# Linformer attention and a gated FFN on one core: the value projection of 14 of 16 token blocks by seven products of half-size matrices

## The chip, the cores and the metric

One NeuronCore of a Trainium2 chip runs the whole program in one launch. The metric is the device time of one execution in microseconds (us). The engines are TensorE (PE in the profile, its weight loads PEld), VectorE (DVE), ScalarE (ACT), GpSimd (POOL) and SyncE (SP); POOL and SP also issue the transfers (DMAs).

## The reference

Attention with K and V projected along the sequence to 64 rows, then a gated feed-forward layer; in the kernel's terms:

```python
k_proj = np.einsum('ks,bhsd->bhkd', E, k)          # 8 batches, 8 heads, 1024 tokens, 64 wide
v_proj = np.einsum('ks,bhsd->bhkd', F, v)
attn = softmax(q @ k_proj.T / 8)                   # over the 64 projected rows
x = (attn @ v_proj).transpose(0, 2, 1, 3).reshape(8192, 512)
gate = 1.0 / (1.0 + np.exp(-(x @ w_gate)))         # 512 -> 1536
out = (gate * (x @ w_val)) @ w_out                 # 1536 -> 512
```

Inputs and output are float32; the matmuls run on bf16 operands with float32 sums.

## The kernel before, in words

The 8192 tokens are 16 **blocks** of 512, two to a batch. xT holds the attention output of a batch transposed (four chunks of 128 rows, two blocks), hT the hidden layer of a block (twelve chunks m of 128 rows by 512 tokens), wG, wV and wO the weights.

For each m, `mstep` makes four matmuls of 512 columns for the gate and four for the value, each group into a PSUM bank of its own. `gate` has ACT take tanh of half the gate sum into sig, and DVE make (sig + 1) x value into hT; the missing factor 0.5 comes with the output.

The output projection of blocks 1 to 14 is made by **seven products** instead of eight (Winograd's form of Strassen's scheme): hT and wO are cut into two by two parts, sums of parts (`s_sums` into hS and in place in hT, `t_sums` into wT) are multiplied, and partial results are read out of the running sums in PSUM by `keep_snap` (ACT) and `add_snap` (DVE). `first_products` makes five products into two banks, `last_products` the other two. Blocks 0 and 15 use the straight `oproj`.

The attention of batch b+1 is cut into pieces (`scores`, `mixed`, `outputs` and so on) that are placed at fixed spots among the msteps of batch b. exp goes to eT; the sums over it come as a matmul with a pattern (dsel); DVE makes reciprocals (`rec`) into rden; `gather` moves them by four small DMAs on SP into rows of rrow (the memory of eT); `spread` has POOL broadcast each row over the partitions into rb, sixteen instructions per batch; `mul` multiplies xu by rb into xT on DVE. K, V and q of batch b+2 are loaded on POOL's queue; q and the projected K are transposed by DMAs on SP.

The order of every engine's work is the order in which the program emits it. `Plan.add` finds for each operation the writers and readers of the keys it names, and the engine waits for their semaphores; a PSUM bank is one key, so its users on different engines take turns. Between matmuls there is no wait on PE itself. `Ring` hands banks out in turn: four for the FFN, four for attention.

Of the kernel before, what the change touches and what calls it, by code (L numbers as in the profile page):

```python
# [7 lines left out]
ALU = mybir.AluOpType  # L8
# [4 lines left out]
P = 128  # L13
# [105 lines left out]
def bass_linformer_attn__then__ffn_glu_sigmoid_kernel(  # L119
# [18 lines left out]
    with contextlib.ExitStack() as es:  # L138
# [5 lines left out]
        count = sbuf("count", [P, P], FP32)  # L144
        quad = sbuf("quad", [P, 1], FP32)
        row_f = sbuf("row_f", [P, 1], FP32)
        pats = sbuf("pats", [P, 4, 32], FP32)
        rows = sbuf("rows", [P, 4, 32], FP32)
        half = sbuf("half", [P, 2], FP32)
        identf = sbuf("identf", [P, P], FP32)  # L150
        ident = sbuf("ident", [P, P], BF16)
        dsel = sbuf("dsel", [P, 2, 2, 32], BF16)
        dsel8 = sbuf("dsel8", [P, 2, 4, 32], BF16)
        bsel8 = sbuf("bsel8", [P, 4, 2, 64], BF16)
        bsel8f = sbuf("bsel8f", [P, 4, 2, 64], FP32)
# [5 lines left out]
        KV = [sbuf(f"KV{i}", [P, H, S // P * DH], BF16) for i in range(2)]  # L161
        kp = sbuf("kp", [P, NR, DH], BF16)
# [5 lines left out]
        rden = sbuf("rden", [P, 512], FP32)  # L168
        rhi = sbuf("rhi", [P, 512], BF16)
        rhl = sbuf("rhl", [P, 512], BF16)  # L170
# [4 lines left out]
        rb = sbuf("rb", [P, 8, 512], FP32)  # L175
# [6 lines left out]
        sig = [sbuf(f"sig{i}", [P, 512], FP32) for i in range(3)]  # L182
# [4 lines left out]
        snap = [EF[:, 0:512], EF[:, 512:1024], sbuf("snap2", [P, 512], FP32)[:, :]]  # L187

# [28 lines left out]
        ffn, att = Ring(FB), Ring(AB)  # L217

# [119 lines left out]
        def constants():  # L338
# [61 lines left out]
            for t, k, m, w in ((dsel8, "dsel8", 8, 4), (dsel, "dsel", 4, 2)):  # L400
# [131 lines left out]
        def half_unit(hf, ring):  # L532
# [86 lines left out]
            def bc(R):  # L619
# [17 lines left out]
                def keep(g):  # L637
                    act(
                        rb[:, 2 * R + g, :],
                        bank[bks[g]][:, :],  # L640
                        [],
                        [("rb", 2 * R + g)],
                        b=bks[g],
                    )
# [17 lines left out]
            def xo(R):  # L662
# [14 lines left out]
                for g in range(2):  # L677
                    n = 2 * R + g
                    if hf:
                        act(xu[:, n, :], bank[bks[g]][:, :], [], [("xu", n)], b=bks[g])  # L680
                    elif R == 0:
                        scale(R, g, bank[bks[g]], rb[:, n, :], [("rb", n)], bks[g])
                if hf == 0 and R == 1:
                    for r in (2, 3):
                        for g in range(2):
# [5 lines left out]
                                    rb[:, 2 * R + g, cc],  # L691
                                    ALU.mult,
                                ),
                                [("rb", 2 * R + g)],
# [57 lines left out]
        def keep_vd(bk):  # L752
            for g in range(2):
                act(
                    vpD[64 * g : 64 * g + 64, :, :].rearrange("p h d -> p (h d)"),
                    bank[bk][64:128, :],
                    [],
                    [("vpD", h, g, R) for h in range(2) for R in range(2)],
                    b=bk,
                )  # L760

        def attention(b):
# [39 lines left out]
            def den():  # L802
                bk = att.next()
                for rnd in range(2):
                    for j in range(4):
                        n = 4 * rnd + j
                        mm(
                            bk,
                            bank[bk][32 * j : 32 * j + 32, :],
                            dsel[:, n % 2, rnd, :],  # L810
                            eT[:, n, :],
                            [("dsel", n % 2), ("eT", n)],
                            start=(rnd == 0),
                            stop=(rnd == 1),
                            tp=(0, 32 * j),
                        )
                den_bank.append(bk)

# [9 lines left out]
            def den8():  # L828
                bk = att.next()
# [51 lines left out]
            def gather():  # L881
                for i in range(4):
                    add(
                        "SP",
                        lambda e, i=i: e.dma_start(rrow[::32, i, :], rden[i::32, :]),
                        r=[("rden", c, R) for c in range(4) for R in range(2)],
                        w=[("rrow", i)] + [("eT", 2 * i + x) for x in range(2)],
                        dma=f"rrow{i}",
                    )

            def spread(rnd):
                for j in range(4):
                    n = 4 * rnd + j
                    for c, parts in ((1, P), (0, 64)):
# [4 lines left out]
                            r=[("rrow", 2 * rnd + c)]  # L899
                            + [("eT", 4 * rnd + 2 * c + x) for x in range(2)],  # L900
                            w=[("rb", n)],
# [21 lines left out]
            def mul(r, g, bk=None):  # L923
# [9 lines left out]
                    [("xu", n)] + ([("rb", n)] if bk is None else []),  # L933
# [13 lines left out]
            def scores():  # L947
                f, a0, a1 = two(ffn), two(att), two(att)
                order = (0, 1, 2) if b == 1 else (2, 0, 1)
# [15 lines left out]
            def outputs():  # L965
# [4 lines left out]
                if 2 < b + 1 < B:  # L970
                    held["kv"] = att.next()
                    kv(b + 1, held["kv"])
                den8() if b == 1 else den()
# [3 lines left out]
            if b == 1:  # L977
# [13 lines left out]
            return [  # L991
                scores,
                lambda: exp_one(1, held["sc"]),
                mixed,
                lambda: keep_x(1, held["x"]),
                outputs,
                lambda: (keep_x(3, held["x"]), rec(1)),
                lambda: (rec(2), keep_kd(held["kv"]) if b + 1 < B else None),
                lambda: (rec(3), gather(), keep_vd(held["kv"]) if b + 1 < B else None),
                lambda: (spread(0), spread(1)),  # L1000
                lambda: mul2(0),
                lambda: mul2(1),
                lambda: mul2(2),
                lambda: mul2(3),
            ]
# [50 lines left out]
        def gate(blk, m, pg, pv):  # L1056
# [3 lines left out]
                sg[:, :], bank[pg][:, :], [], [("sig", M % 3)], b=pg, func=AF.Tanh, scale=0.5  # L1060
# [4 lines left out]
                    sg[:, :],  # L1065
# [5 lines left out]
                [("sig", M % 3)],  # L1071
# [4 lines left out]
        def oproj(blk, tt, pb, cols=((0, DM),)):  # L1076
            o = ost[:, tt, :]
            t = 2 * (2 * (blk % 2) + tt % 2) + tt // 2
            for n, (c0, c1) in enumerate(cols):
                if n:  # L1080
                    pb = ffn.next()
# [17 lines left out]
                )  # L1099
                add(  # L1100
# [24 lines left out]
        def s_sums(blk, n, ms):  # L1125
# [11 lines left out]
            dve(  # L1137
                lambda e: e.tensor_tensor(o, a, b, op),  # L1138
                [k for x in r.split() for k in part(blk, x, up)],
                [k for k in part(blk, w, up)],  # L1140
# [32 lines left out]
        def keep_snap(n, bk):  # L1173
            act(snap[n], bank[bk][:, :], [], [("snap", n)], b=bk, scale=0.5)
# [23 lines left out]
        def first_products(blk):  # L1198
            a, c = ffn.next(), ffn.next()
# [5 lines left out]
            for ms in ((0, 3), (3, 6)):  # L1205
                s_sums(blk, 4, ms)
# [5 lines left out]
            add_snap(2, c, 1, 1)  # L1212

        def last_products(blk):
# [6 lines left out]
            ffn.next(), ffn.next()  # L1221
            for tt in (2, 3, 0, 1):
# [6 lines left out]
                )  # L1229

# [61 lines left out]
        def sums(blk, m):  # L1292
            if m >= 9 and 1 <= blk < 2 * B - 1:
                s_sums(blk, m - 8, (0, 3))
            if m <= 2 and blk >= 2:
                s_sums(blk - 1, m + 1, (3, 6))
            if blk == 2 and m <= 3:
                t_sums(m)

        for b in range(B):  # L1300
            todo = []
            for blk in (2 * b, 2 * b + 1):
                ms = [[m] for m in range(NF)]
                if blk <= 1:
                    ms = [[0, 1]] + ms[2:]
                gaps = {11: [0, 1, 2, 3]} if blk == 1 else {}
                for m in ms:
                    if len(m) == 2:
                        todo.append(
# [89 lines left out]
```

The softmax here doesn't subtract the row's maximum and nothing guards it: scores larger than these inputs give would overflow.

## Time and profile before

| | |
|---|---|
| three runs | 546.61, 546.85, 547.0 us; median 546.85 |
| the profiled execution | 547.47 us, its span from first to last instruction 545.4 us |
| granted TensorE clock | 1.0 |
| wide matmuls of gate and value | 768 each, mean record 379 ns (they overlap) |
| POOL broadcasts into rb | 96, 77.1 us busy |
| DVE gates (L1063) | 192, 130.6 us busy |
| ACT tanh (into sig) | 192, 116.1 us busy |
| DVE sums for hS and hT (L1138) | 112 of 128x768 bf16, about 65 us busy |
| DMA | 56.09 MB, mean 103 GB/s |

A group of instructions is given by line, engine, operation, written and read tiles, and shape (partitions x elements). Matmul records overlap, so their pitch is read from start to start. Idle time of an engine that is not the one that sets the end costs nothing. Line 227 is the helper that records every matmul, line 231 the one for every ACT instruction.

### The profile page before, as it was taken

What the parts mean: (1) busy time and instruction counts of PE and PEld (TensorE: products, weight loads), DVE (VectorE), ACT (ScalarE), POOL (GpSimd) and SP (SyncE); (2) the same over time, 40 slices, a digit from 0 to 9 for tenths busy, and PEclk for the clock granted to TensorE, in tenths of its full rate; (3) what the DMA queues carried; (4) which work ended last, traced back from release to release, by engine and by line L of the source; (5) the groups of instructions that cost most, each with busy time, mean ns of one, the idle gap of its engine ahead of it and who ended that gap; (6) DMA issues with size and microseconds to landing.
All of it is one profiled execution on the core that took longest, in us unless ns stands there. A gap on an engine that the chain in (4) does not pass through costs nothing.

```text
span 545.4 us, 8923 instructions
## 1 busy us (share of the span) xinstructions
PE 530.7 (97%) x3504; PEld 298.7 (55%) x3561; DVE 305.5 (56%) x499; ACT 232.1 (43%) x414; POOL 113.5 (21%) x148
## 2 busy tenths in 40 slices
PE   5999999999999999999999999999999999999998
PEld 4544445646565474644647465564656547474654
DVE  4645386346863559437583466734785375834432
ACT  2654823465335633365333753346533562323330
POOL 9310200103800055000830019000350007100000
PEclk9999999999999999999999999999999999999999
DMA  9999998983795117960286502953020202001022
GB/s 159 200 195 201 163 209 176 153 178 49 148 201 127 31 21 150 152 156 11 79 137 131 121 12 78 185 144 59 13 78 1 78 0 81 2 7 72 1 77 78
DMA packets 76570, 56.09 MB, mean 103 GB/s; under 512 B 34704, under 2 KB 68240, under 8 KB 76528
## 3 DMA queue, kind: packets, MB, share of 16 engines
q0 software_dynamic: 33984, 29.89, 35.4%
q1 hardware_dynamic: 42544, 25.63, 18.6%
q8 instruction: 28, 0.46, 0.4%
q14 instruction: 14, 0.11, 0.1%
HBM read 60.29 MB, written 16.78 MB: 141 GB/s over the span
## 4 chain that ended last, share of the span: by engine, by line
PE 93%; DMA 2%; DVE 1%; ACT 1%; issue 1%; POOL 1%; POOLq 0%
PE pF L227 88%; PE pA L227 5%; DMA KV<-in_v_dram 2%; DVE hT L1063 0%; DVE rden L822 0%; POOL KV L245 0%; POOL Qb L245 0%; ACT xu L231 0%; ACT vpD L231 0%; ACT sig L231 0%; ACT eT L231 0%; ACT kpd L231 0%; DVE rden L602 0%; DVE hS L1138 0%; DVE xT L651 0%
## 5 line engine op out<-in xcount | busy, mean ns | idle before, releaser
L1063 DVE SCALAR_TENSOR_TENSOR hT<-sig,pF 128x512 bf16<-128x512 f32 x192 | 130.6, 681 | 118.9 <-PE pF L227 75.1
L227 PE MATMUL pF<-xT,wV 128*128 128x512 bf16 x752 | 195.6, 379 | 1.2 <-DVE hT L1063 0.3
L227 PE MATMUL pF<-xT,wG 128*128 128x512 bf16 x729 | 191.2, 379 | 3.1 <-issue 1.3
L231 ACT ACTIVATE sig<-pF 128x512 f32<-128x512 f32 x192 | 116.1, 605 | 171.2 <-PE pF L227 146.6
L896 POOL PARTITION_BROADCAST rb<-eT x96 | 77.1, 864 | 279.6 <-DMA eT<-rden 274.5
L227 PEld LDWEIGHTS pF<-xT,wV 128*128 128x128 bf16 x768 | 75.0, 98 | 90.9 <-DVE hT L1063 1.0
L227 PEld LDWEIGHTS pF<-xT,wG 128*128 128x128 bf16 x768 | 72.6, 98 | 88.6 <-issue 9.0
L227 PE MATMUL pF<-wO,hT 128*128 128x256 bf16 (+3 forms) x610 | 80.8, 287 | 0.1
L227 PEld LDWEIGHTS pF<-wO,hT 128*128 128x128 bf16 x612 | 59.2, 98 | 19.7 <-issue 0.8
L1183 DVE SCALAR_TENSOR_TENSOR ost<-pF,EF 128x512 f32<-128x512 f32 x28 | 19.4, 692 | 51.4 <-PE pF L227 48.8
L227 PE MATMUL pF<-wT,hT 128*128 128x256 bf16 x336 | 41.2, 273 | 0.0
L927 DVE TENSOR_TENSOR xT<-xu,rb 128x512 bf16<-128x512 f32 x48 | 40.3, 878 | 0.0
L227 PE MATMUL pF<-wT,hS 128*128 128x256 bf16 x336 | 39.0, 273 | 0.3 <-ACT EF L231 0.3
L231 ACT ACTIVATE EF<-pF 128x512 f32<-128x512 f32 x28 | 16.7, 597 | 47.0 <-PE pF L227 46.9
L227 PEld LDWEIGHTS pF<-wT,hT 128*128 128x128 bf16 x336 | 32.9, 98 | 6.8
L227 PEld LDWEIGHTS pF<-wT,hS 128*128 128x128 bf16 x336 | 32.8, 98 | 4.3 <-ACT EF L231 0.6
L822 DVE RECIPROCAL rden<-pA 128x128 f32<-128x128 f32 x26 | 24.6, 950 | 9.5 <-PE pA L227 9.5
L1183 DVE SCALAR_TENSOR_TENSOR ost<-pF,snap 128x512 f32<-128x512 f32 x14 | 9.7, 692 | 35.6 <-PE pF L227 25.0
L231 ACT ACTIVATE xu<-pA 128x512 f32<-128x512 f32 x46 | 25.2, 617 | 1.1 <-PE pA L227 1.1
L231 ACT ACTIVATE snap<-pF 128x512 f32<-128x512 f32 x14 | 8.4, 597 | 28.3 <-PE pF L227 28.3
L231 ACT ACTIVATE eT<-pA 128x512 bf16<-128x512 f32 x35 | 19.3, 622 | 1.0 <-PE pA L227 1.0
L231 ACT ACTIVATE eT<-pF 128x512 bf16<-128x512 f32 x29 | 15.8, 594 | 8.3 <-PE pF L227 8.2
(93 smaller groups left out, 268.5 us busy)
## 6 DMA issues: line engine op xcount, KB each, us to landing
out_dram<-ost SPq DMA_DIRECT2D x63, 256.0 KB, 2.4
Qb<-in_q_dram POOLq DMA_DIRECT2D x7, 1024.0 KB, 17.8
KV<-in_k_dram POOLq DMA_DIRECT2D x7, 1024.0 KB, 9.8
KV<-in_v_dram POOLq DMA_DIRECT2D x7, 1024.0 KB, 14.0
wO<-in_moe_w_out_dram POOLq DMA_DIRECT2D x1, 1536.0 KB, 11.9
wG<-in_moe_w_gate_dram POOLq DMA_DIRECT2D x5, 256.0 KB, 18.2
wV<-in_moe_w_val_dram POOLq DMA_DIRECT2D x5, 256.0 KB, 18.8
KV<-in_k_dram POOLq DMA_DIRECT2D x2, 512.0 KB, 8.8
```

The costliest lines, as they stand in the source:

```text
L227: return add("PE", lambda e: e.matmul(o, lhsT, rhs, **kw), r=r, x=[("bank", b)])
L231: return add("ACT", lambda e: e.activation(o, i, func, scale=scale), r=r, w=w, x=x)
L822: lambda e: e.reciprocal(rden[:, cc], bank[bk][:, cc]),
L896: lambda e, n=n, i=2 * rnd + c, j=j, parts=parts: e.partition_broadcast(rb[0:parts, n, :], rrow[32 * j : 32 * j + 1, i, :], channels=parts),
L927: lambda e: e.tensor_tensor(xT[s][:, r, :, 256 * g : 256 * g + 256], xu[:, n, :].rearrange("p (f c) -> p f c", f=2), y.rearrange("p (f c) ...
L1063: lambda e: e.scalar_tensor_tensor(hT[blk % 2][:, m, :], sg[:, :], 1.0, bank[pv][:, :], ALU.add, ALU.mult,),
L1183: lambda e: e.scalar_tensor_tensor(o, bank[bk][:, :].rearrange("p (j c) -> p j c", j=2), 0.5, snap[n].rearrange("p (j c) -> p j c", j=2), ...
```

## The change

**Values by seven products.** From block 2 on the value projection too is cut in two by two by two: two halves of the tokens (256 each), two halves of the 512 inputs, two halves of the 1536 outputs. Sums of parts of wV are made once by `vt_sums` (T1 in place in wV, T2 to T4 in the new vT); sums of parts of xT per block by `xs_sums` into xS, both on DVE. `v_product` is one product for a pair of m: four matmuls of 256 columns.

**Units.** The work is in units K of four gate groups (`g_step`) and seven value products (`v_pieces`), six units per batch, each laid out in nine slots: `p3` of the unit before, `p1`, gate, `p26`, gate, `p57`, gate, `p4`, gate of the next unit. Two PSUM banks a and c of a unit take running sums; ACT copies them to vsnap (`v_snap`), DVE adds the other bank (`v_add`), and `hidden` on DVE makes hT from sig and vsnap, in one of four cases from PSUM. Banks come from free lists (FF, AA) instead of rings.

**Sums on GpSimd.** S1 to S3 of the output products of blocks 2 to 14, which DVE made before, are made on POOL: three instructions of 128x1024 elements after the second unit of a block (four of the six chunks of a half), three of 128x512 after the third; for block 2b both come ahead of the `spread` of the same pass on POOL's queue, for block 2b+1 the first comes behind it. A key q7 keeps them apart from broadcasts. S4 stays on DVE.

**Attention.** Its parts get spots at slots (u, j), u the unit and j the slot: `scores` at (0, 0), `mixed` at (1, 0), `outputs` at (3, 0), with the later ACT copies one bank at a time (`late`). The denominators of all batches use the layout that batch 1 had (`den8`: two `rec` of 128 columns instead of four, eight gather DMAs instead of four). `mul` sits in the output products at (5, 0), two before and one behind them, and at (5, 4).

**Memory.** rb shares the memory of the K and V tiles; constants used only at the start, and others, share that of vT.

Batch 0 stays as it was, apart from four straight `oproj` of block 0 at its end, where the sums for weights and block 1 are made.

```diff
+        KVs = sbuf("KVs", [P, 2, H, S // P * DH], BF16)
+        KV = [KVs[:, i, :, :] for i in range(2)]
+        rb = (
+            KVs[:, :, :, :].rearrange("p w h c -> p (w h c)").bitcast(FP32)
+            .rearrange("p (n c) -> p n c", n=8)
+        )
...
             def gather():
-                for i in range(4):
+                for m in range(8):
...
-                            w=[("rb", n)],
+                            w=[("rb", n), ("KV", n // 4, n % 4 // 2)],
...
+            def outputs3():
+                f, a0 = FF.two(), AA.two()
+                xo_one(2, f)
+                xo_one(3, a0)
+                bd = AA.take()
+                den8(bd)
+                if b + 1 < B:
+                    held["kv"] = AA.take()
+                    kv(b + 1, held["kv"])
+                for g in range(2):
+                    x_half(2, g, f)
+                    FF.append(f[g])
+                later("A0", x_half, 3, a0, AA)
+                rec(0)
+                rec(1)
+                AA.append(bd)
+                gather()
+                spread(0)
+                spread(1)
...
-            for ms in ((0, 3), (3, 6)):
-                s_sums(blk, 4, ms)
+            s_sums(blk, 4, (0, 6))
+            hook(0)
             product(blk, a, "S2", "T2")
             keep_snap(1, a)
             product(blk, c, "S1", "T1", True)
             product(blk, a, "A21", "T3")
             keep_snap(2, a)
             add_snap(2, c, 1, 1)
+            hook(1)
...
+        def hidden(K, half_, tok, x, r, b=None):
...
+            o = hT[blk % 2][:, m : m + 2, cc]
+            dve(
+                lambda e: e.scalar_tensor_tensor(
+                    o,
+                    sg[:, :, cc],
+                    1.0,
+                    x.rearrange("p (j c) -> p j c", j=2),
+                    ALU.add,
+                    ALU.mult,
+                ),
...
+        def v_snap(n, bk):
+            act(vsnap[n][:, :], bank[bk][:, :], [], [("vsnap", n)], b=bk)
+
+        def v_add(n, bk):
+            o = vsnap[n][:, :]
+            dve(
+                lambda e: e.tensor_tensor(o, bank[bk][:, :], o, ALU.add),
...
+            def p1():
+                held_v["a"] = a = FF.take()
+                v_product(blk, q, a, "A11", "B11", start=True)
+                v_snap(0, a)
+
+            def p26():
+                a = held_v["a"]
+                held_v["c"] = c = FF.take()
+                v_product(blk, q, c, "A12", "B21", start=True, stop=True)
+                v_add(0, c)
+                v_product(blk, q, a, "S2", "T2")
+                v_snap(1, a)
+                hidden(K, 0, 0, vsnap[0][:, :], [("vsnap", 0)])
+
+            def p57():
+                a, c = held_v["a"], held_v["c"]
+                v_product(blk, q, c, "S1", "T1", start=True)
+                v_product(blk, q, a, "S3", "T3")
+                v_snap(2, a)
+                v_add(2, c)
+
+            def p4():
+                a = held_v["a"]
+                v_product(blk, q, a, "A22", "T4", stop=True)
+                hidden(K, 0, 1, bank[a][:, :], [], b=a)
+                FF.append(a)
+                hidden(K, 1, 1, vsnap[2][:, :], [("vsnap", 2)])
+
+            def p3():
+                c = held_v["c"]
+                v_product(blk, q, c, "S4", "B22", stop=True)
+                v_add(1, c)
+                FF.append(c)
+                hidden(K, 1, 0, vsnap[1][:, :], [("vsnap", 1)])
...
+        for i, fn in zip((12, 14, 15, 16, 17, 18, 19, 19, 20, 21, 22), attention(1)):
+            put(i, fn)
...
+        put(22, lambda: [s_sums(1, n, (3, 6)) for n in (1, 2, 3)])
+        put(22, lambda: (vt_sums(3), vt_sums(1), vt_sums(2), vt_sums(4)))
+        put(23, lambda: (t_sums(0), t_sums(1)))
+        put(24, lambda: (t_sums(2), t_sums(3)))
+        put(25, lambda: [xs_sums(2, n) for n in (1, 2, 3, 4)])
...
+            if b > 1:
+                on(0, 2, lambda: pool_sums(o0, (4, 6)))
+            on(2, 4, lambda: pool_sums(o1, (0, 4)))
+            on(3, 0, lambda: pool_sums(o1, (4, 6)))
+            if b + 1 < B:
+                on(5, 4, lambda: pool_sums(o1 + 1, (0, 4)))
+            on(2, 0, lambda: [xs_sums(o1 + 1, n) for n in (1, 2, 3, 4)])
+            k0 = 0 if b == 1 else 2
+            on(k0, 0, lambda: first_products(o0))
+            on(k0, 2, lambda: last_products(o0))
...
+                on(5, 0, lambda: first_products(o1, hook))
+                on(5, 4, lambda: (mul(3, 0), mul(3, 1)))
+                on(5, 7, lambda: [xs_sums(o1 + 2, n) for n in (1, 2, 3, 4)])
...
+            on(5, 2, lambda: last_products(o1))
+            if b + 2 < B:
+                on(0, 4 if b == 1 else 2, lambda: (load_k(b + 2), load_v(b + 2), load_q(b + 2)))
+                on(3, 4, transpose_q)
```

(o0 is block 2b - 1 and o1 block 2b of the pass for batch b; `hook` multiplies r = 0 and 1 at its first call, r = 2 at its second.)

## The prediction

> **What bounds the kernel now.** I read the busy shares and the chain first, then the sums over single batch pairs, then the order of instructions in one quiet stretch, then how long one line's instructions last.
>
> ```profile
> PE 530.7 (97%) x3504; PEld 298.7 (55%) x3561; DVE 305.5 (56%) x499; ACT 232.1 (43%) x414; POOL 113.5 (21%) x148
> PE 93%; DMA 2%; DVE 1%; ACT 1%; issue 1%; POOL 1%; POOLq 0%
> 187.92:252.51 64.59, 64.12 (x409) 36.59 (x416) 37.91 (x58) 28.92 (x52) 15.36 (x19) 1.00 0.50 101
> 252.51:317.10 64.59, 64.11 (x409) 36.59 (x416) 37.93 (x58) 28.92 (x52) 15.37 (x19) 1.00 0.50 101
> ```
>
> The last two lines are two passes of the loop over batches: the length, then the busy time of PE, PEld, DVE, ACT, POOL, then the granted clock. The pass is 64.59 us each time and PE is busy for 64.1 of it at full clock. So TensorE sets the end, and it hardly waits. Only fewer columns through PE can help, and every wait that PE gets is paid in full.
>
> The price of columns, and of a hand-over, is in the timeline of a quiet stretch (start, length, engine, line):
>
> ```profile
> 280.46 1.03 PE L227 MATMUL pF<-xT,wG 128*128 128x512 bf16 x4
> 281.32 1.03 PE L227 MATMUL pF<-xT,wV 128*128 128x512 bf16 x4
> 281.58 0.60 ACT L231 ACTIVATE sig<-pF 128x512 f32<-128x512 f32 x1 [1.13 <-PE pF L227]
> 282.19 1.03 PE L227 MATMUL pF<-xT,wG 128*128 128x512 bf16 x4
> 282.46 0.69 DVE L1063 SCALAR_TENSOR_TENSOR hT<-sig,pF 128x512 bf16<-128x512 f32 x1 [0.57 <-PE pF L227]
> 287.37 2.78 PE L227 MATMUL pF<-wO,hT 128*128 128x256 bf16 x24
> 289.99 0.27 PE L227 MATMUL pF<-wT,hS 128*128 128x256 bf16 x1
> ```
>
> Four 512-column matmuls start every 0.862 us (280.46, 281.32, 282.19), so a wide matmul costs 0.2155. Twenty-four 256-column ones take 289.99 - 287.37 = 2.62 us, 0.109 each: half width costs half. After a group ends, ACT starts 0.26 us later (281.32 to 281.58) and DVE 0.27 (282.19 to 282.46).
>
> **The gain.** A block's values were 48 wide matmuls, 48 x 0.2155 = 10.34 us. Seven products of 2 x 6 matmuls of 256 columns are 84 x 0.109 = 9.16. That is 1.18 less per block, 14 blocks: **-16.5 us**. Gate, output products, scores and K/V projection keep their columns. The denominators go from 8 wide matmuls to 16 of half width, four side by side as before: no change.
>
> **What ACT and DVE get.** Per pass of two blocks there are six units; each adds three snapshots on ACT (0.60) and three additions on DVE. DVE instructions of 128x512 that follow one another start every 0.60 us. ACT goes from 28.9 to 28.9 + 18 x 0.60 = 39.7 us, DVE from 37.9 by +18 x 0.60, +8 x 0.35 for xS (a 128x768 bf16 sum lasts 0.55, so by elements 0.37 and less in a row), -12 x 0.47 for the sums that leave, -2 x 0.9 for two reciprocals, to about 44. Both fit in a pass of some 62.2 us. What matters is the order inside a unit: 28 x 0.109 + 16 x 0.2155 = 6.5 us of PE.
>
> **Hand-overs in a unit.** The tightest is `p4`: it adds to bank a after `v_snap(2)` has read it, covered by one gate group, 0.862 us. The snapshot costs 0.26 + 0.60, and PE has started 0.05 us after an ACT or DVE end where it waited (96.15 to 96.20): 0.91, so 0.05 per unit, 42 x 0.05 = 2.1 us. In three units per pass the `late` halves of exp and xu stand ahead of it on ACT and make it about 0.1 more, 18 x 0.1 = 1.8. The others have room: `S1 T1` waits for `v_add(0)`, ready at 2.0, done at 2.7, wanted at 3.0; `p3` for `v_add(2)`, done at 5.5, wanted at 6.1. Together **+4**; from 0 (ACT and PE overlap by that 0.05) to 17, if each unit loses 0.4.
>
> **The seam after batch 0.** The four straight output groups of block 0 last 4 x 2.59 = 10.4 us. Behind the last gate DVE gets there: 8 multiplications by 0.60, 5 sums by 0.47, four `vt_sums` and four `t_sums` of 128x1536 at 0.87 apart (the 0.95 us row), four evictions, four xS sums: 4.8 + 2.4 + 7.0 + 2.4 + 1.5 = 18, and waits for the first eviction make it 19. `add_snap(0)` of the next output products queues behind that and ends at 19.8; PE wants its bank at 10.4 + 0.6 + 0.9 + 3 x 1.31 = 15.8. **+4**, once; 0 to 6.
>
> **The port.** The sums S1 to S3 go to POOL, and no row of before has a TENSOR_TENSOR there. What POOL does to DVE is in these lines (minimum, median, maximum of a line, then DVE's and POOL's timeline):
>
> ```profile
> L927 DVE TENSOR_TENSOR xT<-xu,rb x48: 681/792/1147, 140.0 to 471.0; 128x512 bf16<-128x512 f32 x48
> L927 DVE TENSOR_TENSOR xT<-xu,pA x8: 677/680/681, 74.1 to 81.3; 128x512 bf16<-128x512 f32 x8
> L1063 DVE SCALAR_TENSOR_TENSOR hT<-sig,pF x192: 624/687/690, 25.3 to 532.4; 128x512 bf16<-128x512 f32 x192
> 269.18 1.97 DVE L927 TENSOR_TENSOR xT<-xu,rb 128x512 bf16<-128x512 f32 x2
> 272.70 2.14 DVE L927 TENSOR_TENSOR xT<-xu,rb 128x512 bf16<-128x512 f32 x2
> 276.16 1.29 DVE L927 TENSOR_TENSOR xT<-xu,rb 128x512 bf16<-128x512 f32 x2
> 268.22 6.21 POOL L896 PARTITION_BROADCAST rb<-eT  x7 [0.16 <-POOL rb L896]
> L896 POOL PARTITION_BROADCAST rb<-eT x96: 794/799/1207, 131.6 to 465.4; - x96
> ```
>
> Two multiplications take 1.29 us when POOL is quiet, 1.97 and 2.14 while broadcasts run (until 274.4); the broadcast itself stretches from 0.80 to 1.21. The same multiplication with one input in PSUM never exceeds 0.681, and the gates, also with one PSUM input, not 0.690. So a DVE instruction with two SBUF inputs and a POOL instruction exclude each other. After the change three of a unit's four `hidden`, all xS sums, S4 and the multiplications by rb are of that kind.
>
> [...]
>
> Price of a sum of 1024 bf16 elements on POOL, D: not below 0.8, the broadcast that writes the same 2 KB per partition; not above 3.2, twice for the elements (1024 for 512) and twice for the second input. By bytes alone 0.8, by elements alone 1.6; I take **1.2**, half way.
>
> Most places have cover. At (2,4) the sums wait for `S1 T1` of the output products (hS is one buffer), which puts them under 8 us of output products where DVE has only PSUM work. The half-size sums at (0,2) and (3,0) run under scores and `outputs`. The spread meets `hidden` six times, 0.3 us each, inside DVE's slack.
>
> The place without cover is slot (5,0), six passes. Counted from there, PE wants `add_snap(2)` done at 9.6 (p3, five output products of 1.31, p1, a gate group, one product) and `v_add(0)` at 12.65. The spread starts late: rec ends 3.9 us after (3,0), eight gather DMAs instead of four at about 0.6 each on SP (four take 2.36 us) put the first broadcast 4.8 us behind it, and 16 x 0.775 plus 2 us of collisions end it at 7.4 after (5,0); then S1 to S3 start. DVE has `hidden` to 2.2, `add_snap(0)` to 3.9, S4 to 5.1, three multiplications to 7.8 among the broadcasts; the fourth waits for S1 (port free 0.3 before its end). With D = 1.2: fourth to 9.2, `add_snap(2)` 9.8 (0.3 late with the hand-over), the next two 10.65 and 12.1 between S2 and S3, `add_snap(1)` and `v_add(0)` 13.3 against 12.95: 0.7 per pass, **+4**. With D = 0.8 nothing is late; 1.6: 1.85, +11; 2.4, midway to the upper bound: 4.2, +25; 3.2: 6.8, +41. Behind the three sums POOL has the next half-size sums and loads, some 9 us of slack later.
>
> **K and V under rb.** Loads of batch b+2 wait for POOL's half-size sums, so go out some 6 us into the pass; V lands 14 us after issue, Q 17.8, and `outputs` wants K and V some 31 us in. Nothing, with 11 us to spare; without that cover PE would stand for the rest of the load. On SP the transposes of q stand behind 2.4 us more of gather, a pass ahead of the scores: nothing.
>
> **Edits without a price.** Four constants of 0.34 us leave DVE at the start, where the chain waits for K and V instead; `keep` writes xu in place of rb. At the end `hidden(1,0)` comes two DVE instructions after p3, 1.5 us, under the first ten matmuls of the straight output group (2.2 us); without them PE would wait that long.
>
> **The sum**, against the profiled execution's span of 545.4: 545.4 - 16.5 + 4 + 4 + 4 = 540.9. The median of the runs, 546.85, is 1.5 above that span: **542.5 us**.
>
> **The rivals.** *Everything is covered*: D near 0.8, no hand-over late, the seam within its slack; 545.4 - 16.5 + 1.5 = 530.4, up to 534. For it: the broadcasts cost PE nothing now. Against: DVE's 19 us of work in 11 at the seam. 0.12.
> *The port decides* (slower): at slot (5,0) POOL's three large sums lock out the multiplications, and PE stands for `add_snap(2)` and `v_add(0)`. The gain is gone once a pass loses (16.5 - 8)/6 = 1.4 us, from D of about 1.5. At 1.6: 549; at 2.4: 563; at the upper bound 579; its likeliest part 549 to 565. For it: the stretched rows; against: POOL's speed is not seen. 0.30.
> *The hand-overs eat it*: seven banks per unit change between PE, ACT and DVE, and 0.4 us lost in each of 42 units is 16.8: 546 to 550, no change or slightly slower. For it: three covers of about 0.86 us; against: ACT's starts are regular to 0.01 us. 0.14, half of it within the measurement.
>
> **How the numbers follow.** Forecast, 534 to 545.7: 0.44. A measurement of this kernel tells 0.2%, 1.1 us, from no change. Faster 0.44 + 0.12 = 0.56, same 0.07, slower 0.30 + 0.07 = 0.37. The range, 531 to 563, leaves out the low end of full cover and a D above 2.4. The forecast's own range is 534 to 546.
>
> **What would show it.** Right: passes of about 62.5 to 64 us, PE busy nearly throughout; POOL TENSOR_TENSOR 128x1024 of 1.2 us; PE's only waits on DVE at (5,0) and the seam. Wrong: a POOL sum above 1.5 us with `xT<-xu,rb` rows of 1.5 us and PE waiting on `ost` or `vsnap`; or ACT's snapshots as PE's releaser in each unit.

## The result, and the profile after

The changed kernel took **578.58 us** (573.99 to 584.19 in four runs) against 546.92 us for the kernel before: 1.0551 times as long, 95% interval 1.049 to 1.0612. Ratios, here and below, leave out executions that took over 1.5% longer than the fastest of their kernel. The forecast of 542.5 us was wrong, and on the wrong side: the kernel got slower. The profiled execution took 578.65 us, its span 576.8.

The page of the changed kernel: busy shares, the granted clock in 40 slices, and the chain that ended last.

```profile
PE 533.1 (92%) x4113; PEld 348.1 (60%) x4113; DVE 401.2 (70%) x577; ACT 300.9 (52%) x540; POOL 263.2 (46%) x226
PEclk9999999988999999899998999999997999999999
PE 71%; DVE 16%; DMA 8%; issue 3%; POOL 1%; SPq 1%; ACT 0%; DVEq 0%; POOLq 0%
```

PE no longer sets the end alone: DVE holds 16% of the chain and DMA 8%, where before they held 1% and 2%. The clock is no longer full throughout: 0.979 in the mean, for 1.000 before, and below 0.9 in five of the 40 slices.

Stretches of about one pass each, from the end of `outputs` in one pass, slot (3, 0), to its end in the next (length, then busy time of PE, PEld, DVE, ACT, POOL, clock, DMA share, GB/s):

```profile
141.76:205.54 63.78, 62.78 (x497) 43.09 (x498) 49.82 (x69) 38.70 (x69) 38.54 (x32) 1.00 0.51 102
205.54:273.06 67.52, 64.43 (x499) 43.65 (x498) 50.15 (x69) 38.60 (x69) 38.02 (x32) 0.97 0.49 97
273.06:341.78 68.72, 63.96 (x497) 43.66 (x498) 51.38 (x69) 38.60 (x69) 37.88 (x32) 0.98 0.49 95
341.78:406.39 64.61, 62.96 (x497) 43.02 (x498) 51.01 (x69) 38.65 (x69) 39.29 (x32) 1.00 0.53 100
406.39:474.91 68.52, 63.62 (x481) 43.40 (x482) 49.99 (x67) 38.33 (x69) 33.29 (x27) 0.95 0.19 50
```

Before, each pass took 64.59. One pass is faster than that, one the same, three are 3 to 4 us slower, at a clock below 1. Ahead of them something else went wrong: block 4's first gate already starts 18.2 us later than before (169.45 for 151.28), of 31.4 at the end.

**A slow pass.** POOL's, DVE's and PE's timelines of the changed kernel around the first gates of block 8 (start, length, engine, line, in brackets the idle time before):

```profile
288.10 7.38 POOL L916 PARTITION_BROADCAST KVs<-eT  x7 [0.19 <-POOL KVs L916]
302.78 2.19 POOL L1226 TENSOR_TENSOR hS<-hT 128x1024 bf16<-128x1024 bf16 x1 [7.29 <-DVE xS L1372]
305.05 2.18 POOL L1226 TENSOR_TENSOR hS<-hS,hT 128x1024 bf16<-128x1024 bf16 x1
307.30 2.18 POOL L1226 TENSOR_TENSOR hT<-hT 128x1024 bf16<-128x1024 bf16 x1
...
302.57 0.42 DVE L1372 TENSOR_TENSOR xS<-xS,xT 128x512 bf16<-128x512 bf16 x1
302.91 2.34 DVE L1372 TENSOR_TENSOR xS<-xT 128x512 bf16<-128x512 bf16 x1
305.17 2.33 DVE L1372 TENSOR_TENSOR xS<-xT,xS 128x512 bf16<-128x512 bf16 x1
307.43 0.68 DVE L1429 TENSOR_TENSOR vsnap<-pF,vsnap 128x512 f32<-128x512 f32 x1
308.14 1.89 DVE L1410 SCALAR_TENSOR_TENSOR hT<-sig,vsnap 128x512 bf16<-128x512 f32 x1
...
302.88 0.61 PE L263 MATMUL pF<-xT,wV 128*128 128x256 bf16 x4
308.16 1.89 PE L263 MATMUL pF<-xT,wG 128*128 128x512 bf16 x4 [4.68 <-DVE vsnap L1429]
```

Read it from the bottom. PE stands 4.7 us until `v_add(1)` (L1429, from 307.43) has freed a bank. That addition is held up by nothing of its own: two xS sums ahead of it take 2.34 and 2.33 us instead of 0.42, each until a POOL sum of 2.18 has ended. POOL's sums stand there because POOL was idle for 7.3 us between its last broadcast (ends 295.5) and its first sum. Had it gone on at once, these three would have ended at about 302.2, when xS begins. The gate's four matmuls then take 1.89 us instead of 1.03: from 308.2 to 311.2 the granted clock is 0.54.

**The first pass.** SP, POOL and PE in the changed kernel's timeline:

```profile
106.39 1.46 SPq L779 DMA_TRANSPOSE kpD<-kpd  x1
...
104.57 0.89 POOL L281 DMA_DIRECT2D KVs<-in_k_dram  x1 [31.96 <-PE pF L263]
...
108.70 0.60 PE L263 MATMUL pF<-xS,wV 128*128 128x256 bf16 x4
115.34 0.64 PE L263 MATMUL pF<-qT,kpD 64*64 64x512 bf16 x4 [6.04 <-DMA kpD<-kpd]
116.77 1.04 PE L263 MATMUL pF<-xT,wV 128*128 128x256 bf16 x4
```

The stretch of that wait and the one behind it, columns as above:

```profile
109.00:115.30 6.30, 0.30 (x3) 0.02 (x1) 1.71 (x3) 0.90 (x2) 0.00 (x0) 0.81 1.21 189
115.30:118.30 3.00, 2.96 (x18) 1.26 (x19) 0.00 (x0) 1.49 (x3) 0.00 (x0) 0.50 1.24 208
```

The scores wait 6.0 us (6.04 in the row) for the small transposition of the projected K. It was issued at 106.39, behind the loads of batch 3 (from 104.57), and landed 8.9 us later; the median of the six is 3.2. In the kernel before it was issued at 94.63 and the loads at 96.72. The clock is then 0.50 for 3 us. Ahead of this lies a wait of 3.51 us for `add_snap(0)` (L1278), and behind it one of 4.72 us for `vsnap`:

```profile
94.09 1.48 PE L263 MATMUL pA<-wT,hS 128*128 128x256 bf16 x12 [3.51 <-DVE ost L1278]
133.56 1.03 PE L263 MATMUL pF<-xS,wV 128*128 128x256 bf16 x4 [4.72 <-DVE vsnap L1429]
```

Waits of PE are given here as the idle time in its rows. Those that the expectations name are up to 0.2 us longer, since they count from where the next matmul could have started.

How long one instruction lasts, by groups of the changed kernel (busy us, mean ns, then idle before them):

```profile
L1226 POOL TENSOR_TENSOR hS<-hT 128x1024 bf16<-128x1024 bf16 x13 | 28.3, 2178 | 117.0 <-PE pA L263 54.2 <-DVE xS L1372 30.2 <-DVE hT L1410 17.8
L1226 POOL TENSOR_TENSOR hT<-hT 128x1024 bf16<-128x1024 bf16 x13 | 29.1, 2240 | 1.0
L1410 DVE SCALAR_TENSOR_TENSOR hT<-sig,vsnap 128x512 bf16<-128x512 f32 x126 | 112.8, 895 | 5.8
L1410 DVE SCALAR_TENSOR_TENSOR hT<-sig,pF 128x512 bf16<-128x512 f32 x42 | 28.9, 687 | 0.7 <-PE pF L263 0.7
```

D, the price of a POOL sum, is 2.2 us, not 1.2. The same `hidden` costs 687 ns with one input in PSUM and 895 in the mean with two in SBUF (731 in e1 below, with no sums on POOL): the lock that the prediction read out of the multiplications. It calls it the port; the rows show that the two engines keep each other out, not by what. DVE has 50 to 51 us of work a pass in the table of stretches, where the prediction had about 44; the lock is part of that (18 `hidden` with two inputs in SBUF a pass, 0.21 us longer each than with one in PSUM, are 3.7 us).

### The profile page after: what moved, and what is told of

It is laid out like the page before. It is cut to its first block, busy times and chain, and to the rows that moved or that the text cites. A ratio compares the mean times of both kernels' runs of the same rounds, so it can differ in the third digit from the quotient of the medians.

```text
span 576.8 us, 10389 instructions
## 1 busy us (share of the span) xinstructions
PE 533.1 (92%) x4113; PEld 348.1 (60%) x4113; DVE 401.2 (70%) x577; ACT 300.9 (52%) x540; POOL 263.2 (46%) x226
## 4 chain that ended last, share of the span: by engine, by line
PE 71%; DVE 16%; DMA 8%; issue 3%; POOL 1%; SPq 1%; ACT 0%; DVEq 0%; POOLq 0%
PE pF L263 50%; PE pA L263 21%; DVE xT L948 5%; DVE xS L1372 4%; DMA Qb<-in_q_dram 3%; DVE vsnap L1429 3%; DMA KVs<-in_v_dram 2%; DVE hT L1410 2%; DMA kpD<-kpd 2%; DVE ost L1278 1%; SPq L741 1%; DMA out_dram<-ost 1%; POOL KVs L281 1%; DVE hT L1226 1%; ACT vsnap L267 0%
## 5 line engine op out<-in xcount | busy, mean ns | idle before, releaser
L1429 DVE TENSOR_TENSOR vsnap<-pF,vsnap 128x512 f32<-128x512 f32 x126 | 86.6, 687 | 68.6 <-PE pF L263 46.4
L1410 DVE SCALAR_TENSOR_TENSOR hT<-sig,vsnap 128x512 bf16<-128x512 f32 x126 | 112.8, 895 | 5.8
L267 ACT ACTIVATE vsnap<-pF 128x512 f32<-128x512 f32 x126 | 75.2, 597 | 67.2 <-PE pF L263 60.6
L916 POOL PARTITION_BROADCAST KVs<-eT x96 | 88.0, 943 | 43.3 <-PE pF L263 29.5
L263 PE MATMUL pF<-xT,wV 128*128 128x256 bf16 (+1 forms) x432 | 78.1, 303 | 0.3 <-DVE hT L1149 0.3
L263 PE MATMUL pA<-wO,hT 128*128 128x256 bf16 x504 | 59.7, 273 | 2.3 <-DVE ost L1278 2.1
L263 PE MATMUL pF<-xS,wV 128*128 128x256 bf16 x336 | 51.3, 276 | 7.1 <-DVE vsnap L1429 7.0
L263 PEld LDWEIGHTS pA<-wO,hT 128*128 128x128 bf16 x504 | 48.7, 98 | 10.0 <-DVE ost L1278 4.2
L263 PE MATMUL pF<-xS,vT 128*128 128x256 bf16 x336 | 51.9, 278 | 0.0
L1226 POOL TENSOR_TENSOR hS<-hS,hT 128x1024 bf16<-128x1024 bf16 (+1 forms) x26 | 47.1, 1811 | 2.0
L1278 DVE SCALAR_TENSOR_TENSOR ost<-pA,EF 128x512 f32<-128x512 f32 x28 | 19.3, 688 | 28.0 <-PE pA L263 28.0
## 6 DMA issues: line engine op xcount, KB each, us to landing
Qb<-in_q_dram POOLq DMA_DIRECT2D x7, 1024.0 KB, 18.2
wG<-in_moe_w_gate_dram POOLq DMA_DIRECT2D x5, 256.0 KB, 19.2
```

The source lines that it names most:

```text
L263: return add("PE", lambda e: e.matmul(o, lhsT, rhs, **kw), r=r, x=[("bank", b)])
L267: return add("ACT", lambda e: e.activation(o, i, func, scale=scale), r=r, w=w, x=x)
L916: lambda e, n=n, i=2 * rnd + c, j=j, parts=parts: e.partition_broadcast(rb[0:parts, n, :], rrow[32 * j : 32 * j + 1, i, :], channels=parts),
L1278: lambda e: e.scalar_tensor_tensor(o, bank[bk][:, :].rearrange("p (j c) -> p j c", j=2), 0.5, snap[n].rearrange("p (j c) -> p j c", j=2), ...
L1410: lambda e: e.scalar_tensor_tensor(o, sg[:, :, cc], 1.0, x.rearrange("p (j c) -> p j c", j=2), ALU.add, ALU.mult,),
L1429: lambda e: e.tensor_tensor(o, bank[bk][:, :], o, ALU.add),
```

## The experiments

Unless another base is named, each is an edit of the changed kernel. Ratios are to the kernel before on the same chip, with 95% intervals. "Block 2 to 3" is the time between the first gate matmuls of those blocks: 37.1 us before, 51.8 in the changed kernel.

**e1, all sums on DVE.**

```diff
-                    s_sums(blk, n, ms, "POOL")
+                    s_sums(blk, n, ms)
```

> S1 to S3 of blocks 2 to 14 go back to DVE at the same places; nothing else changes. Theory port (POOL's sums of 2.2 us, late by a change of code after the spread, hold the port while xS sums and hidden wait, and PE stands behind them): DVE rows with two SBUF inputs go back to 0.68 (hidden) and 0.42 (xS) outside the spread, the PE gaps of 1.0 to 4.9 us at the end of each pass go to under 0.5, passes from 63.8 to 68.7 become 62.5 to 64, the time is 555 to 562. Rival DVE load (DVE simply has too much work at 50 of 64 us per pass): 6 us more work per pass on DVE make passes longer than 67 us, the time 580 or more.

Measured 567.93 us, 1.037 (1.0353 to 1.0387). Taking POOL out gains about 1.8% of the time before, some 10 us, less than expected. The passes behind the first are now alike, 65.5 us at clock 1.00, with waits of 0.76 (for `mul(3)`, behind three sums at (5,4)) and 1.29 us (for `vsnap`) in each. POOL's part is shown, but something else loses on DVE.

**e2, e1 with POOL's change between additions and broadcasts kept.** Two-element additions on POOL at the places of the sums, reading the parts of hT that the sums read.

```diff
+                    pool(
+                        lambda e: e.tensor_tensor(scr[:, 0:2], scr[:, 2:4], scr[:, 2:4], ALU.add),
+                        r=part(blk, "A21", range(*ms)) + part(blk, "A22", range(*ms)) + ["scr"],
```

> As the run with the sums on DVE, but POOL still makes, at each former place of a sum, an addition of two elements per partition, so that it still changes between code for additions and for broadcasts twice per pass, and holds the port for hardly any time. Port theory: within 1% of the run with the sums on DVE. Rival, the change of code itself disturbs (its transfer, or the loads of K and V that start later behind it): 4 us or more per pass slower than that run, 25 us in all.

Measured 589.92 us, 1.0775 (1.0745 to 1.0805). The size is the rival's, but it tells nothing of the theories: S3 overwrites A21, so DVE waited for the small addition behind the idle time on POOL (19.2 us in six waits, the longest 4.6). It shows what happens when DVE does wait for it.

**e6, the same without that dependency** (r = S2 of those chunks, which nothing overwrites soon; three additions at each place).

> All sums on DVE as in e1, and at each former place of the sums on POOL three two-element additions on POOL, which nobody waits for. POOL changes its code as often as in the changed kernel but holds nothing for long. Theory, that the change of code costs PE only through what waits behind it on the port: within 1% of e1, 565 to 573. Rival, that the 13 us of code changes per pass hurt by themselves (late broadcasts, late loads): 4 us or more per pass, above 590.

Measured 569.76 us, 1.0413 (1.039 to 1.0436), passes of 65.5 as in e1. POOL in e6 (start, length, idle before):

```profile
289.61 0.98 POOL L918 PARTITION_BROADCAST KVs<-eT  x1
297.44 0.73 POOL L1623 TENSOR_TENSOR scr<-scr 128x2 bf16<-128x2 bf16 x3 [6.85 <-DVE xT L950]
302.79 0.85 POOL L1623 TENSOR_TENSOR scr<-scr 128x2 bf16<-128x2 bf16 x3 [4.62 <-DVE hS L1228]
```

Three additions of next to nothing start 6.85 us after the last broadcast, nearly as late as the real sums. By itself this row does not say why: they read sums that DVE finished only at 295.5, so up to 4.9 us of it can be that wait. The changed kernel does say it. What its first sum at 302.78 needs was there when the last broadcast ended at 295.5: DVE had made those parts of hT by 288.3, and PE had read hS for the last time by 291.5. There the idle time belongs to the change between the two kinds of instruction; in e6 the rest of 1.9 us does, since the second three additions, with no broadcast before them, start 0.09 us after the DVE sum that they read, as a sum of the changed kernel that follows other sums starts 0.08 us after its `hidden` (202.61 to 202.69). The kernel pays 0.4% for it. By itself the change is cheap; it matters by where it puts the sums.

**e4, xS ahead of POOL's sums.**

```diff
-                on(5, 7, lambda: [xs_sums(o1 + 2, n) for n in (1, 2, 3, 4)])
+                on(5, 4, lambda: [xs_sums(o1 + 2, n) for n in (1, 2, 3, 4)])
```

> The xS sums for the next pass move from (5, 7) to (5, 4), right behind the last multiplications, so that DVE makes them before POOL's first large sum. Port theory: xS sums take 0.42 us each at that place, the PE gap behind them shrinks by 2 to 4 us in the passes that had 3 to 5, the time falls by 6 to 15 us; hidden still meets the large sums. Rival, xS sums are not what PE waits for: no change within 1%.

Measured 568.63 us, 1.0382 (1.0361 to 1.0402). Nearly as much as e1 gains (9 us for 10) comes from moving four DVE sums of 0.42 us out of the way of three POOL sums: this collision alone costs that much.

**e7, POOL for one of two blocks.** Sums of block 2b, ahead of the broadcasts, stay on POOL; those of 2b+1 go to DVE.

```diff
-                    s_sums(blk, n, ms, "POOL")
+                    s_sums(blk, n, ms, "POOL" if blk % 2 == 0 else "DVE")
```

> Sums of the first block of a pass (ahead of the broadcasts) stay on POOL, those of the second (behind the broadcasts) go to DVE. Theory, that only the second block's sums hurt, since they meet the sums xS and the hidden layer: 560 to 569, at or a little below e1. Rival, that any sum of 2.2 us on POOL costs its share: half way between e1 and the changed kernel, 571 to 575.

Measured 572.68 us, 1.0465 (1.0445 to 1.0485), as the rival would have it. But the passes are 65.3 to 65.5 us, those of e1. More than the whole difference to e1 lies in the first pass: block 2 to 3 takes 53.6 us instead of 45.0, since there hS is free early and the sums run under xS (the wait of 4.72 us is back). The first pass was not in the theory.

**e3, loads placed later.**

```diff
-                on(0, 4 if b == 1 else 2, lambda: (load_k(b + 2), load_v(b + 2), load_q(b + 2)))
+                on(1 if b == 1 else 0, 2, lambda: (load_k(b + 2), load_v(b + 2), load_q(b + 2)))
```

> In the first pass alone the loads of K, V and q of batch 3 are issued at (1, 2) instead of (0, 4). Theory crowding (the transposition of the projected K lands 8.9 us after issue instead of 2.7 because these loads stand ahead of it): it lands in about 3 us, the PE gap of 6.2 us before the scores goes to under 1, the time falls by 6 to 8 us, to about 571. Rival, the transposition is late because of SP's own queue: no change, 578.

Measured 575.73 us, 1.0505 (1.0455 to 1.0556), not to be told from the changed kernel. The loads still went out at 103.9: POOL had nothing ahead of them in its queue, and a later place in the emission is no wait. The edit did not do what it was meant to.

**e5, loads made to wait.**

```diff
-                r=turned() if b >= 2 else (),
+                r=turned() + ([("kpD", 0)] if b == 3 else []) if b >= 2 else (),
```

> The changed kernel with one more wait: in the first pass the load of K for batch 3 waits until the transposition of the projected K (kpD) has landed. Theory, that this transposition lands 8.9 us after its issue only because the loads were issued just ahead of it: it lands in about 3 us, the gap of 6.2 us before the scores falls below 1, the time falls by 6 to 8 us to about 571. Rival, that the transposition is slow for another reason (the crowd of small transfers): gap and time unchanged, 576 to 579.

Measured 566.09 us, 1.023 (1.0147 to 1.0313); the four runs go from 556.01 to 569.48, and the profile is of the longest. Block 2 to 3 falls from 51.8 to 37.5 us, twice what was expected: the slow clock and the later collision in that pass go with the wait. The later passes of this one profile swing: waits of 6.6 us for `vsnap` in two of them, 0.8 in two others. In a pass of 72.6 us the first sum on POOL starts at 224.74 and three xS sums behind it take 2.3 us each; in one of 64.1 us xS has ended at 298.4, 0.1 us before the first sum.

**e8, e1 with the sums of 2b+1 made in the next pass.**

```diff
-                on(0, 2, lambda: pool_sums(o0, (4, 6)))
+                on(0, 3, lambda: pool_sums(o0, (0, 4)))
+                on(1, 3, lambda: pool_sums(o0, (4, 6)))
...
-            if b + 1 < B:
-                on(5, 4, lambda: pool_sums(o1 + 1, (0, 4)))
```

> All sums on DVE as in e1, but those of the second block of a pass are made in the next pass ((0,3) and (1,3)) instead of among the output products at (5,4). Theory, that what is left per pass in e1 (0.92 us of waiting for xT and 1.45 for vsnap, 65.5 us a pass) is DVE's backlog at that one place: passes of 62.5 to 63.5, time 551 to 558. Rival, that DVE is too full wherever they stand: passes stay near 65.5, time 565 to 570.

Measured 555.08 us, 1.0145 (1.0127 to 1.0163), passes of 63.7 to 63.8. What e1 lost in each pass was for the most part the place (5,4). DVE is as busy as in e1 (51.1 us a pass) and has room.

**e9, e8 with the wait of e5.**

> e8 with the wait of e5 (load of K for batch 3 behind the transposition of the projected K). Theory, that the 6.0 us before the scores of the first pass come from the loads ahead of that transposition, and the slow clock after it is their consequence: the stretch from the start of block 2 to that of block 3 falls from 45.5 us to 37 to 38.5, the time to 546 to 549. Rival, that e5's gain was an accident of how its sums on POOL then fell: at most 3 us, 552 or more.

Measured 546.93 us, 1.0001 (0.9991 to 1.0011), block 2 to 3 in 37.5 us (45.4 in e8). SP, POOL and PE of e9:

```profile
104.51 1.19 SPq L779 DMA_TRANSPOSE kpD<-kpd  x1
...
108.09 0.88 POOL L281 DMA_DIRECT2D KVs<-in_k_dram  x1 [44.62 <-PE pA L263]
...
107.35 0.41 PE L263 MATMUL pF<-qT,kpD 64*64 64x512 bf16 x4
```

With no load ahead of it the transposition has landed within 2.8 us, since the scores that read it start at 107.35, with no wait in front of them. This is worth 1.44% of the time before, 8 us, against 5.85 us of wait in e8. The clock was 0.50 for 3 us behind that wait, which makes up some 1.5 of the rest.

**e10, e9 with three more moves on DVE and SP.**

```diff
-        put(24, transpose_q)
+        put(25, transpose_q)
-        put(22, lambda: (vt_sums(3), vt_sums(1), vt_sums(2), vt_sums(4)))
-        put(23, lambda: (t_sums(0), t_sums(1)))
-        put(24, lambda: (t_sums(2), t_sums(3)))
-        put(25, lambda: [xs_sums(2, n) for n in (1, 2, 3, 4)])
+        put(22, lambda: (vt_sums(3), vt_sums(1)))
+        put(23, lambda: t_sums(0))
+        put(24, lambda: t_sums(1))
+        put(25, lambda: t_sums(2))
+        def seam(i):
+            if i == 0:
+                t_sums(3)
+                for n in (1, 2):
+                    xs_sums(2, n)
+            else:
+                vt_sums(2)
+                vt_sums(4)
+                for n in (3, 4):
+                    xs_sums(2, n)
...
+                on(0, 0, lambda: [xs_sums(o1, n) for n in (3, 4)])
...
-            on(k0, 0, lambda: first_products(o0))
+            on(k0, 0, lambda: first_products(o0, *([seam] if b == 1 else [])))
...
-                on(5, 7, lambda: [xs_sums(o1 + 2, n) for n in (1, 2, 3, 4)])
+                on(5, 7, lambda: [xs_sums(o1 + 2, n) for n in (1, 2)])
```

> e9 with three more moves, all on DVE: the sums for weights and xS that stood ahead of the first add_snap of batch 0's end go behind it; the transposition of q goes behind the last output transfer there; xS's third and fourth sum go behind the value addition of the next pass's first slot, where PE waited 1.0 us a pass. Theory, that DVE's order is the whole rest: the 3.7 and 1.5 us of the seam go, passes of 63.75 fall to about 62.8, 536 to 542, faster than before. Rival, that DVE is full and the waits only move: 545 to 549.

Measured **538.57 us**, 0.9832 (0.9816 to 0.9847): faster than both kernels. The page of e10:

```profile
PE 523.6 (97%) x4113; PEld 344.5 (64%) x4113; DVE 401.8 (75%) x655; ACT 300.6 (56%) x540; POOL 124.9 (23%) x148
PEclk9999999999999999999999999999999999999999
PE 79%; DVE 14%; DMA 4%; issue 2%; POOL 1%; ACT 0%; DVEq 0%; POOLq 0%
```

Two passes of e10 by windows:

```profile
212.50:275.60 63.10, 62.85 (x499) 43.14 (x497) 51.15 (x81) 38.59 (x70) 17.38 (x19) 1.00 0.57 105
275.60:338.60 63.00, 62.76 (x498) 43.03 (x496) 51.04 (x81) 38.49 (x70) 17.48 (x19) 1.00 0.54 101
```

The same 4113 matmuls keep PE busy 9.5 us less than in the changed kernel (523.6 for 533.1), most of it because they run at full clock (an estimate: five stretches of 3 us at about half clock make some 7.5 us), and PE's share is back at 97%. Of e9's waits, the 3.51 us at the seam is gone and the 0.83 in each pass is under 0.4; the three moves were not tried one by one. The values by seven products are a gain once nothing stands in their way, by 8 us.

**e11, e10 with all of its sums S1 to S3 back on POOL.**

```diff
-                    s_sums(blk, n, ms)
+                    s_sums(blk, n, ms, "POOL")
```

> e10 with all of the sums S1 to S3 on POOL again, at the places of e10 (2b+1 in the next pass at (0,3) and (1,3), 2b at (2,4) and (3,0)). Theory, that a sum of 2.2 us on POOL locks out the hidden layer wherever that is due: 2 to 4 us a pass more than e10, 550 to 562. Rival, that only the place behind the broadcasts was wrong and sums on POOL are free elsewhere: within 1% of e10.

Measured 566.77 us, 1.0356 (1.0319 to 1.0393): 28 us more than e10. POOL's first sum of a pass in e11's timeline:

```profile
303.37 2.53 POOL L1226 TENSOR_TENSOR hS<-hT 128x1024 bf16<-128x1024 bf16 x1 [8.21 <-PE pA L263]
```

What PE waited for in e11 (us in total over the span, times, longest):

```profile
PE pA L263 <- DVE ost L1278: 11.4, 10, 2.6
PE pA L263 <- POOL hS L1226: 7.6, 4, 3.1
PE pF L263 <- DVE vsnap L1429: 4.2, 9, 1.5
```

The size was as expected, the way only half: the lock is there (a `hidden` of 2.21 us, xS sums of 1.37 and 1.25), but PE also waits for the sums themselves. Behind 8.2 us of idle POOL they start at 303.4 and end at 315.3, while the products want hS from 312.9.

**e12, e10 with one block's sums on POOL**, where output products cover them.

```diff
-                    s_sums(blk, n, ms)
+                    s_sums(blk, n, ms, "POOL" if blk % 2 == 0 and blk > 2 else "DVE")
```

> e10 with the sums of one block of each pass (2b, from block 4 on) on POOL, at (2,4) and (3,0), which is ahead of the broadcasts and under output products. Theory, that a sum of 2.2 us on POOL costs only where PE or DVE's work with two SBUF inputs is due: passes of 63.1 us as in e10, time within 0.4% of e10, 537 to 541. Rival, that every sum on POOL costs its share: half of e11's 4.7 us a pass, 549 to 555.

Measured 537.91 us, 0.9835 (0.982 to 0.985), the same as e10. One pass of e12 by windows, and the first sum in its timeline:

```profile
212.50:275.60 63.10, 62.74 (x499) 43.15 (x498) 49.44 (x75) 38.63 (x70) 28.04 (x25) 1.00 0.55 104
```
```profile
235.89 2.12 POOL L1226 TENSOR_TENSOR hS<-hT 128x1024 bf16<-128x1024 bf16 x1 [19.79 <-PE pA L263]
```

POOL works 10.7 us more per pass than in e10 and DVE 1.7 less, and neither changes the pass: a POOL sum of 2.1 us was free at this place, where DVE has PSUM work and PE other work. It also brings nothing, since DVE has that slack anyway.

## Why the prediction was wrong

**The gain held; the hand-overs cost less, and elsewhere.** PE's rows in a unit of e10:

```profile
219.02 1.03 PE L263 MATMUL pF<-xT,wG 128*128 128x512 bf16 x4
219.88 0.60 PE L263 MATMUL pF<-xT,vT 128*128 128x256 bf16 x4
220.32 0.81 PE L263 MATMUL pF<-xT,wG 128*128 128x512 bf16 x3
```

A product's four matmuls take 0.44 us (219.88 to 220.32), 0.109 each as reckoned, so the 16.5 us of columns are saved, and DVE and ACT have room in every pass, as was said. The hand-over at `p4` (xT,vT) was to cost 0.05 us in each unit and 0.1 more in some, +4 in all. Here it costs nothing, 0.86 us behind the gate group, as in 36 of e10's 42 units, and 0.3 us in all. Instead PE loses 0.33 us a pass to a `v_add` and 0.24 to an output addition. The pass was to be 62.9 us (2.36 less for columns, 0.65 more for hand-overs) and is 63.1 in e10; that these agree so well is partly luck.

**The port's price D was taken too low.** "I take 1.2, half way" stands against 2.18 to 2.24 us measured. Half way between the byte row (0.8) and the element row (1.6) was no argument: even the sums of 512 elements took 1.15 us and more, where a broadcast of 512 had taken 0.80. That the second input counts as well would fit, but no run tries it alone. By the prediction's own steps 2.2 us is worth some 21 us (between +11 at 1.6 and +25 at 2.4), near 560 us, which is in the range of the rival "The port decides". D alone therefore leaves some 19 us of the miss to the steps below. That the rival's upper bound, 579 at D = 3.2, is close to the time measured is chance, since the large sums of the changed kernel take 2.18 to 2.24 us in the mean.

**The place was wrong, too.** The step "16 x 0.775 plus 2 us of collisions end it at 7.4 after (5,0); then S1 to S3 start" had POOL go from a broadcast to a sum at once. It stands idle 7.3 us there. So the sums missed `mul` and `add_snap(2)`, where the collision was worked out, and hit xS and the `hidden` behind it, which the prediction took for free. e4 shows one place of the collision: xS three slots earlier gives some 9 us back. What POOL's sums cost against DVE sums in a good place is 28 us (e10 to e11), 22 from the changed kernel to e8; the prediction had 4.

**"Nothing, with 11 us to spare" failed for the loads.** Only the lateness of K and V was priced, not that a small transposition issued behind their loads would land late (8.9 us after issue, against 2.8 at most in e9). The edit itself moves the loads; that they had stood behind the transposition in the kernel before (96.72 behind 94.63) was there to be read. One pass lost 6.0 us of waiting, 8 us in all (e8 to e9).

**The seam was right**: +4 predicted for `add_snap(0)` behind DVE's backlog, 3.51 measured. The wait of 1.03 us for `add_snap(2)` behind an output transfer that had come late on SP was missed.

**Slow clock was in no step.** After PE's six waits of 2.75 us and more from the seam on the clock was 0.50 to 0.54 for 3 us in all but the first, and PE is busy 9.5 us longer than in e10.

The terms do not add up exactly: 540.9 + 18 (port, 22 for 4) + 8 (loads) + about 5 (seam and xS order beyond the 4 reckoned, from the 9 us of e9 to e10) is 572, and the span was 576.8. Waits in this kernel set off each other, as e5 shows, and the last 5 us stay unassigned.

## What to carry to other kernels

Before work goes to an idle engine, ask three things: how long one instruction there locks the other engine out (2.2 us here), what the engine does between its last kind of work and this one (7.3 us of idle here), and which instructions will stand opposite by then; e12 shows that the same sums cost nothing where the answers are harmless. When a transfer moves, look for the small transfers that it now precedes, and make the order a dependency, since a later place in the program is none (e3 against e5). When matmul work is taken out, the waits that it covered come to light one after the other (e1, e8, e9, e10 gave 10, 12, 8 and 9 us, by the differences of their ratios), so judge the idea after the last of them.

## What the runs showed of the hardware

- **POOL changes its configuration between broadcasts and additions.** The expectations call this a change of code. In the changed kernel two instructions named for it stand on POOL's queue at each change, by source lines (length in ns, then first and last start):

```profile
L1226 POOLq MODIFY_POOL_CONFIG  x14: 64/127/127, 107.3 to 500.6; - x14
L916 POOLq MODIFY_POOL_CONFIG  x12: 8/12/12, 143.1 to 478.1; - x12
```

The trace of before, without sums on POOL, has none at its broadcasts (L896); it has two at 59.1 us, where the program loads the library of the broadcast (L1290). From the last broadcast to the first sum POOL is idle for 7.15 to 7.84 us in the six passes of the changed kernel. Back it is 5.7 to 6.2 us, of which the broadcasts spend a part waiting for the gather (in one pass the reciprocals end at 206.08, its eight transfers are issued from 206.11 to 210.70, the last sum ends at 206.64 and the first broadcast starts at 212.55). One place has no such wait: in e11's first pass the reciprocals end at 124.9 and the last sum at 131.8, and the first broadcast comes 5.96 us later:

```profile
137.76 1.18 POOL L916 PARTITION_BROADCAST KVs<-eT  x1 [5.96 <-PE pA L263]
```

So about 6 us go to the change there, and more than 7 the other way; what POOL does in them, no row shows.
- **The clock.** Stretches of 3 us behind PE's waits in the changed kernel (windows as above):

```profile
94.10:97.00 2.90, 2.90 (x27) 2.61 (x28) 0.80 (x1) 0.08 (x1) 0.00 (x0) 1.00 1.07 206
133.60:136.60 3.00, 3.00 (x12) 1.64 (x13) 1.18 (x2) 0.60 (x1) 0.00 (x0) 0.50 0.00 0
239.10:242.10 3.00, 3.00 (x11) 1.61 (x12) 2.15 (x2) 0.60 (x1) 2.92 (x2) 0.53 0.00 0
```

These follow waits of 3.51, 4.72 and 2.75 us. The length of the wait alone does not decide: behind the same wait at the seam, 3.5 us, the clock over the next 2.9 to 3.1 us was 1.00 in the changed kernel and e8, and 0.63 in e1. What else decides, these runs do not show.
- **Small transposition, large loads.** The same transposition landed in 8.9 us behind loads of 1 MB each and within 2.8 us with no load ahead of it (e9).
